# One core, a state space and gated feed-forward layer with its gradients: loads and stores moved to Sync's queue from the 11th group, and the parameter steps spread anew

## The chip, the cores and the metric

The kernel runs on one core of a Trainium2 chip. The metric is device microseconds of one execution; lower is better. The kernel before takes 1762.47 us, the median of three runs (1759.99 to 1764.7).

## The reference

`reference` is a forward pass with its vector-Jacobian product. With x of 2048 tokens by D = 576, and F = 4608:

```
xn  = layernorm(x)
s   = conv(xn, K) + xn * Dskip        # K[d,l] = Re sum_n C[d,n] exp(dt*A[d,n]*l) dt*B[d,n], causal, by FFT; N = 128
g   = silu( (silu(xn @ w1) * (xn @ w3)) @ w2 )
out = x + s * g
```

It returns out and the gradients for grad_out: of x (out_1), of the state space parameters A, B, C, log_dt and Dskip (out_2 to out_9), and of w1, w3, w2 (out_10, out_11, out_12). All of them are bf16. The part that matters here is the backward pass: with go the gradient at the feed-forward's output, the gradients of the hidden values need go @ w2^T, the weight gradients are products over the 2048 tokens (h^T go for w2, xn^T times the gradients of the gate G and of U for w1 and w3), and the input's gradient is the product of those two with w1^T and w3^T. The gradients of A, B, C and log_dt need sums over time of products of the gradient of K with tables.

## The kernel before, in words

The forward pass comes first and stores the gate G and the up product U in DRAM (`G_dram`, `U_dram`). Then `backward` (line 1521) runs. It has two passes that matter here.

The first is the **gradient pass**, the loop `for gi in range(NG)` at line 1599: 18 groups of FG = 256 columns of F each, counted 0 to 17. The 11th group is gi = 10. A group does the following, in stages that the generator `phase6_group` (1743) names as it yields:

- "h0" to "h3": `make(s)` multiplies go with w2T into `ph` (line 1765), ScalarE copies it (1768), VectorE multiplies it into `gu_n` and `gg_n` (1783), which become the gradients of U and G.
- at "h1" and "h3" `phase6_grad2` (1793) makes the gradient of w2, 128 rows at a time (matmuls at 1806, copies at 1810), and stores it (1811).
- at "h3" the load of `h_n` (U of group gi + 2) is issued (`phase6_load_h`, 1688), into the buffer that this group's second `phase6_grad2` has just read.
- "stored": four stores of `gu_n` and `gg_n` to `GU_dram` and `GG_dram` have been issued on Sync's queue (1788).
- "out_11_0" to "out_10_3", "out_11", "out_10": `phase6_grad13` (1813) makes the gradients of w3 and w1 (1826), each with one store (1832), and the rest of 64 rows each (1836, 1838), whose two stores (`tail`, 1843) are issued when the next group's loads are.
- in between, `phase6_prep` (1724) makes the next group's `gu_n`, `gg_n` and `h_n` ready: ScalarE's Silu and its derivative (1733, 1736), products on VectorE (1729, 1730). It begins at "h3" and reads the load of G, `gg_n` (`phase6_load_gg`, 1704), which is issued with the next group's loads (`phase6_load`, 1709).

The buffers `gg_n`, `h_n` and `gu_n` come in pairs, so group gi + 1 loads where group gi - 1 has been read for the last time.

Into this loop **parameter steps** are mixed (`param_step`, 1230): 36 chunks of 16 channels, two steps a chunk, 72 in all. A step (`param_half`, 1393) is eight matmuls of `qT` with `gz` into `et_ps` (1400), then twice a product with `pz` on VectorE (1405) and a reduction (1408). `et_ps` has three buffers and a step uses two. A chunk's loads (`param_loads`, 1379) are a transpose of `qT`, two loads of `gz` and one of `pz`, all on Sync's queue; after a chunk's second step the chunk two further on is loaded. Steps are taken from gi = GP = 11 on: five a group ("h1", "h3", "out_11", "out_10", "end"), and one more at "stored" in groups 12 to 15. The last group has five. That makes 39; the other 33 lie in the second pass. When 8, 16, 24, 32 and all 36 chunks are done, `phase5_blocks` (1450) finishes blocks of channels, a part at each call of `phase5_step`, with loads and stores on POOL's queue.

The second is the **input pass**, `phase6_inputs` (1852): 16 tiles of 128 tokens, each 72 x 2 matmuls of `acts` (transposed loads of `GG_dram` and `GU_dram`) with w1^T and w3^T (1876). The weights come in by DMA transposes, of which `wA` is loaded at "end" of groups 11 to 15 (`load_wT_rows`, 1673) and the rest in groups 16 and 17 (`load_piece`, 1668). Steps are taken at the places in `stops` (1910).

**The order of the work.** A planner sorts the instructions of each engine by priority (`at`) and by when it thinks their inputs are ready; this order is fixed in the program. Where `issue_after` is used, an instruction stands behind a named one. `gp` and `sc` chain all that goes through them on POOL's and ScalarE's queues. `sp` does so on Sync's queue only while `self.chain` is set, which is from gi = 11 on. A DMA's wait for its data or its buffer is done by the issuing queue, so what stands behind it in that queue waits too. Before the change POOL's queue carries the loads of `gg_n` and `h_n` and all stores of weight gradients; Sync's carries the transposes, the chunk loads, the rows of w2 and the GU/GG stores.

Of the kernel before, what the change touches and what calls it, by code (L numbers as in the profile page):

```python
# [17 lines left out]
P = 128  # L18
# [82 lines left out]
class K:  # L101
# [1128 lines left out]
    def param_step(self):  # L1230
        nch = self.cfg.D // 16
        if self.half == 2 * nch:
            return
        if self.half == 0:
            for ch in range(2):
                self.loaded[ch] = self.param_loads(ch)
        ch, dg = divmod(self.half, 2)
        with self.tc.issue_after(self.pe_last.ins):
            self.param_half(ch, dg, *self.loaded[ch])
        if dg == 1 and ch + 2 < nch:  # L1240
            if self.hold is None:
# [279 lines left out]
    def backward(self, T0, TG, TQ, TC, TX, gctx, mats):  # L1521
        nc, cfg = self.nc, self.cfg
        D, L, LT, F, FT = cfg.D, cfg.L, cfg.LT, cfg.F, cfg.FT
# [9 lines left out]
        FA, GP = 14, 11  # L1533
        with ExitStack() as out:
# [22 lines left out]
            self.tail = None  # L1557
            self.at(T0 - TG)
            gg = self.phase6_load_gg(0, inp)
# [128 lines left out]
    def phase6_load_h(self, gi, T, inp):  # L1688
        self.at(T)
        hn = inp.tile([P, self.cfg.LT, self.FG], BF16, name="h_n")  # L1690
        self.gp(lambda: self.nc.gpsimd.dma_start(out=hn[:], in_=self.U_dram[gi]))
        self.hn[gi] = hn
# [11 lines left out]
    def phase6_load_gg(self, gi, inp):  # L1704
        gg = inp.tile([P, self.cfg.LT, self.FG], BF16, name="gg_n")
        self.gp(lambda: self.nc.gpsimd.dma_start(out=gg[:], in_=self.G_dram[gi]))
        return gg
# [85 lines left out]
    def phase6_grad2(self, gi, fl, hn, gwp, ps_gw):  # L1793
# [6 lines left out]
        if True:  # L1800
# [10 lines left out]
            self.gp(lambda: nc.gpsimd.dma_start(out=aps["out_12"][fi * P:(fi + 1) * P, :], in_=gw2[:]))  # L1811

    def phase6_grad13(self, gi, gg_n, gu_n, gwp, ps_gw):
# [7 lines left out]
        for (nat, oname) in ((gu_n, "out_11"), (gg_n, "out_10")):  # L1821
            gw = gwp.tile([P, nfull, FG], BF16, name="gw13", tag="gw13")
            for c in range(nfull):
# [6 lines left out]
                if (oname, c) in (("out_11", 2), ("out_10", 1)):  # L1830
                    yield oname
            self.gp(lambda: nc.gpsimd.dma_start(out=aps[oname][0:nfull * P, fb:fb + FG].rearrange("(c p) f -> p c f", p=P),
                                                in_=gw[:]))
# [9 lines left out]
        def tail():  # L1843
            self.gp(lambda: nc.gpsimd.dma_start(out=aps["out_10"][nfull * P:D, fb:fb + FG], in_=gw[0:rem, :]))
            self.gp(lambda: nc.gpsimd.dma_start(out=aps["out_11"][nfull * P:D, fb:fb + FG], in_=gw[rem:P, :]))
# [6 lines left out]
    def phase6_inputs(self, T2, TX, wT, acts, pool):  # L1852
# [7 lines left out]
        with pool(name="l_sb", bufs=2) as sb, pool(name="l_s1", bufs=1) as s1, \  # L1860
# [43 lines left out]
            for i in range(LT):  # L1904
# [5 lines left out]
                stops = () if i in (0, 1, LT - 1) else (12, 28, 44, 62) if i == 2 else (14, 38, 62) if i in (3, 4, 6, 8) else (20, 50)  # L1910
# [146 lines left out]
```

## Time and profile before

| | |
|---|---|
| median of three runs | 1762.47 us |
| the profiled execution | 1769.46 us |
| its span, first to last instruction | 1767.7 us |
| TensorE matmul busy | 1638.5 us (93%) |
| VectorE busy | 1357.2 us (77%) |
| ScalarE busy | 937.2 us (53%) |
| POOL busy | 352.2 us (20%) |
| Sync's DMA queue (q1) | 282.62 MB, 63.4% of 16 engines' span |
| POOL's DMA queue (q0) | 107.99 MB, 18.9% |

The profile is one execution. In its rows PE is TensorE's matmuls, PEld its weight loads, DVE VectorE, ACT ScalarE, POOL GpSimd and SP Sync; a q behind the name is the engine's queue or sequencer. A row of instructions begins with the start in us and the time, or with the line and ends with the count; idle time of the engine ahead of an instruction stands in square brackets, with what ended it. A row of a stretch gives its length, then busy us and count of each engine, the granted clock of TensorE, the mean busy share of the DMA engines (packets overlap, so it goes over 1) and GB/s. A row of a wait gives us in total, times, and the longest. A row of a DMA issue gives the count, KB each and the median us from issue to landing. A time written as +n is us after the start of its group, which is the end of the last matmul of line 1838 of the group before.

### The profile page before, as it was taken

The numbers are of one execution on the slowest core, as the hardware profiler recorded it, in microseconds if no ns is written. First come the engines' busy times: TensorE is split into PE (matmuls) and PEld (weight loads), VectorE is DVE, ScalarE is ACT, GpSimd is POOL, SyncE is SP. The second block draws the span as 40 slices with busy tenths as digits, with TensorE's granted clock in tenths as the row PEclk, the third lists the DMA queues.
The fourth block names the chain that finished last, engine by engine and source line by source line (L and its number), as shares of the span: only waits on it lengthen the run. The fifth ranks groups of instructions, "written<-read, shape, count | busy, mean of one in ns | idle before, by whom it ended". The sixth has DMA issues, their size and how long they took to land. (4 is left out here: it accounts for less than half of the span.)

```text
span 1767.7 us, 35373 instructions
## 1 busy us (share of the span) xinstructions
PE 1638.5 (93%) x13849; PEld 1206.2 (68%) x13909; DVE 1357.2 (77%) x2102; ACT 937.2 (53%) x1757; POOL 352.2 (20%) x579
## 2 busy tenths in 40 slices
PE   7789988999999999999989899999789997999998
PEld 2445544544535777788878788888678875778886
DVE  8768888795783554988966989569779975878675
ACT  5789999976863112776746676564444510000101
POOL 3112222223134110111111101111001143031132
PEclk9999999999999999999999999999889998999999
DMA  7889998889699988867664756689989999999992
GB/s 222 271 267 366 348 355 304 305 267 298 224 276 236 227 209 183 223 205 217 192 188 156 221 167 214 176 236 242 183 227 251 207 257 212 227 245 208 236 226 50
DMA packets 634718, 411.98 MB, mean 233 GB/s; under 512 B 424422, under 2 KB 579542, under 8 KB 629942
## 3 DMA queue, kind: packets, MB, share of 16 engines
q1 hardware_dynamic: 579676, 282.62, 63.4%
q0 software_dynamic: 32128, 107.99, 18.9%
q10 hardware_dynamic: 22746, 19.10, 3.9%
q8 instruction: 109, 1.79, 0.4%
q14 instruction: 59, 0.48, 0.1%
HBM read 130.88 MB, written 190.89 MB: 182 GB/s over the span
## 5 line engine op out<-in xcount | busy, mean ns | idle before, releaser
L1876 PEld LDWEIGHTS <-acts 128*128 128x128 bf16 x2304 | 225.9, 99 | 68.5 <-DMA acts<-GU_dram 6.8
L1826 PEld LDWEIGHTS <-xn_bf 128*128 128x128 bf16 x2304 | 224.5, 98 | 47.6 <-issue 21.1
L1405 DVE TENSOR_TENSOR pr_q<-et_ps,pz 128x1024 f32<-128x1024 f32 x144 | 175.8, 1221 | 43.0 <-PE et_ps L1400 36.1
L1876 PE MATMUL px<-wT,acts 128*128 128x288 bf16 x1472 | 189.3, 286 | 0.0
L1032 PEld LDWEIGHTS <-xnT 128*128 128x128 bf16 x1152 | 107.0, 98 | 112.2 <-issue 24.2
L1408 DVE TENSOR_REDUCE S_all<-pr_q 128x32 f32<-128x1024 f32 x144 | 175.1, 1216 | 3.1
L1765 PE MATMUL ph<-w2T,goT 128*128 128x256 bf16 x1440 | 174.6, 275 | 3.1 <-ACT gh L1768 3.1
L1032 PE MATMUL pg<-wmB_w,xnT 128*128 128x512 bf16 x545 | 149.1, 379 | 7.4 <-ACT g_t L1048 4.5
L1765 PEld LDWEIGHTS <-goT 128*128 128x128 bf16 x1440 | 140.6, 99 | 21.6 <-issue 4.5
L1806 PE MATMUL pgw<-go_o,h_n 128*128 128x288 bf16 x1152 | 151.8, 287 | 0.2 <-DVE h_n L1730 0.2
L1826 PE MATMUL pgw<-gu_n,xn_bf 128*128 128x256 bf16 x1152 | 136.8, 274 | 15.0 <-ACT gw L1810 13.3
L1032 PE MATMUL pu<-wmB_w,xnT 128*128 128x512 bf16 x553 | 149.9, 379 | 0.8
L1826 PE MATMUL pgw<-gg_n,xn_bf 128*128 128x256 bf16 x1152 | 130.8, 273 | 1.3 <-ACT gw L1828 1.3
L1806 PEld LDWEIGHTS <-h_n 128*128 128x128 bf16 x1152 | 112.4, 98 | 28.2 <-DVE h_n L1730 0.7
L1768 ACT CAST gh<-ph 128x512 bf16<-128x512 f32 x144 | 82.5, 603 | 89.9 <-PE ph L1765 79.9
L1876 PE MATMUL px<-wA,acts 128*128 128x288 bf16 x832 | 112.2, 293 | 10.2 <-DMA acts<-GU_dram 6.5
L1046 ACT ACTIVATE s_t<-pg 128x512 bf16<-128x512 f32 x144 | 88.0, 611 | 58.0 <-PE pu L1040 32.7
L679 ACT ACTIVATE cs_k<-et_ps 128x512 bf16<-128x512 int16 x216 | 111.6, 640 | 0.7 <-PE et_ps L677 0.7
L1932 ACT ACTIVATE go<-gx 128x576 bf16<-128x576 f32 x16 | 10.9, 683 | 189.7 <-DVE gx L1915 157.8
L1811 POOL DMA_DIRECT2D out_dram<-gw x36 | 19.8, 550 | 381.0 <-ACT gw L1810 200.3
L1729 DVE TENSOR_TENSOR gg_n<-gg_n,h_n 128x1024 bf16<-128x1024 bf16 x72 | 48.8, 683 | 57.0 <-ACT gg_n L1736 57.0
L1060 POOL DMA_DIRECT2D U_dram<-u_t x72 | 51.8, 720 | 203.6 <-ACT u_t L1051 196.7
(317 smaller groups left out, 3272.5 us busy)
## 6 DMA issues: line engine op xcount, KB each, us to landing
U_dram<-u_t POOLq DMA_DIRECT2D x72, 256.0 KB, 4.8
H_dram<-h_t SPq DMA_DIRECT2D x72, 256.0 KB, 4.9
G_dram<-g_t POOLq DMA_DIRECT2D x72, 256.0 KB, 5.0
Q_dram<-q_k SPq DMA_DIRECT2D x36, 512.0 KB, 4.7
gg_n<-G_dram POOLq DMA_DIRECT2D x18, 1024.0 KB, 5.8
h_n<-U_dram POOLq DMA_DIRECT2D x18, 1024.0 KB, 8.8
GG_dram<-gg_n SPq DMA_DIRECT2D x36, 512.0 KB, 10.1
GU_dram<-gu_n SPq DMA_DIRECT2D x36, 512.0 KB, 5.2
```

What stands on the lines that cost most here:

```text
L679: self.sin_last = nc.scalar.activation(out=CS[:, :, o:o + 256], in_=pt[:].bitcast(I16)[:, :, 0::2], func=ACT.Sin, scale=6.283184 / 2 ** 16)
L1032: ins = nc.tensor.matmul(pt[:], lhsT=xnT[:, c, ts], rhs=wm[w][:, c, :], start=(q == 0 and c == 0), stop=(q == 1 and c == nfull - 1))
L1046: nc.scalar.activation(out=s_t[:, :, q, :], in_=pgv, func=ACT.Silu)
L1060: self.u_stores[step] = nc.gpsimd.dma_start(out=dst[fb * ng:(fb + 1) * ng, :, i0:i0 + NT, :].rearrange("g p t f -> p g (t f)"), in_=src[:] ...
L1405: nc.vector.tensor_tensor(out=pr[:].rearrange("p r k e -> p r (k e)"), in0=T[x][:].rearrange("p z k h j a -> p (z k h j a)")[:, None].to_b ...
L1408: nc.vector.tensor_reduce(out=self.S_all[:].rearrange("p r (h c) -> p r h c", h=2)[:, :, :, d0:d0 + 2], in_=pr[:].rearrange("p r k (h j a) ...
L1729: nc.vector.tensor_tensor(out=gg[:, sl, :], in0=gg[:, sl, :], in1=hn[:, sl, :], op=ALU.mult)
L1765: self.pe_last = nc.tensor.matmul(ph[j][:, k, :].rearrange("p (a f) -> p a f", f=P), lhsT=lw, rhs=rh, start=(n == 0), stop=(n == nfull))
L1768: self.sc(lambda: nc.scalar.copy(out=gh[:, j], in_=ph[j][:]))
L1806: self.pe_last = nc.tensor.matmul(pgw[pi_][:, 0:pw], lhsT=hn[:, tt, fl * P:(fl + 1) * P], rhs=go_o[:, tt, po:po + pw], start=(tt == 0), st ...
L1826: self.pe_last = nc.tensor.matmul(pw_[:, 0:FG], lhsT=self.xn_bf[:, tt, c * P:(c + 1) * P], rhs=nat[:, tt, :], start=(tt == 0), stop=(tt == ...
L1876: self.pe_last = nc.tensor.matmul(px[pi_][:, 0:pw], lhsT=acts[i][:, ai, fi, :], rhs=w[:, po:po + pw], start=(n == 0), stop=(n == len(steps ...
```

## The change

From the 11th group on (gi = 10) until the gradient pass ends, a flag `one_queue` is set together with `chain`. While it is set,

- the loads of `h_n` and `gg_n` go to Sync's queue. The load of `gg_n` is kept back until stage "h0" of the group (`gg_due`);
- the stores of out_10, out_11 and out_12 (and the tails) go to Sync's queue through `grad_store`, which puts them on a list; `stores_due` issues the list at the start of the next stage;
- all that goes through `sp` is chained one group earlier, and so w2T is loaded two groups ahead from gi = 10 on.

The loads of the first two chunks are issued at "stored" of gi = 10, not with the first step. Steps are taken at "out_10" and "end" of gi = 10, five times in groups 11 to 16, and five times in the last group; the one at "stored" of groups 12 to 15 is gone. That makes 37. In the input pass tiles 5 and 7 have three stops where they had two: 35.

```diff
@@ param_step
-        if self.half == 0:
-            for ch in range(2):
-                self.loaded[ch] = self.param_loads(ch)
@@ backward
+            self.one_queue, self.gg_due, self.due = False, None, []
...
-                self.chain = gi >= GP
+                self.chain = self.one_queue = gi >= GP - 1
...
                 for stage in group if gi == 0 else self.phase6_group(gi, cur, elp, gwp, ps_h, ps_gw):
+                    self.stores_due()
+                    if stage == "h0" and self.gg_due:
+                        self.gg_due()
+                        self.gg_due = None
...
                     if stage == "stored":
-                        c = gi - GP
-                        if c in (1, 2, 3, 4):
-                            step()
+                        if gi == GP - 1:
+                            for ch in range(2):
+                                self.loaded[ch] = self.param_loads(ch)
...
-                    elif stage in ("h1", "h3", "out_11", "out_10", "end") and gi >= GP and not (lastg and stage in ("out_10", "end")):
+                    elif stage in (("out_10", "end") if gi == GP - 1 else ("h1", "h3", "out_11") if lastg else
+                                   ("h1", "h3", "out_11", "out_10", "end") if gi >= GP else ()):
                         step()
...
+            self.one_queue = False
+            self.stores_due()
@@ phase6_load_h
-        self.gp(lambda: self.nc.gpsimd.dma_start(out=hn[:], in_=self.U_dram[gi]))
+        if self.one_queue:
+            self.sp(lambda: self.nc.sync.dma_start(out=hn[:], in_=self.U_dram[gi]))
+        else:
+            self.gp(lambda: self.nc.gpsimd.dma_start(out=hn[:], in_=self.U_dram[gi]))
@@ phase6_load_gg
+        if self.one_queue:
+            self.gg_due = lambda: self.sp(lambda: self.nc.sync.dma_start(out=gg[:], in_=self.G_dram[gi]))
+        else:
+            self.gp(lambda: self.nc.gpsimd.dma_start(out=gg[:], in_=self.G_dram[gi]))
@@ phase6_grad2 (phase6_grad13 and its tail likewise)
-            self.gp(lambda: nc.gpsimd.dma_start(out=aps["out_12"][fi * P:(fi + 1) * P, :], in_=gw2[:]))
+            self.grad_store(aps["out_12"][fi * P:(fi + 1) * P, :], gw2[:])
+
+    def grad_store(self, out, in_):
+        if self.one_queue:
+            self.due.append(lambda: self.sp(lambda: self.nc.sync.dma_start(out=out, in_=in_)))
+        else:
+            self.gp(lambda: self.nc.gpsimd.dma_start(out=out, in_=in_))
+
+    def stores_due(self):
+        for fn in self.due:
+            fn()
+        self.due = []
@@ phase6_inputs
-                stops = () if i in (0, 1, LT - 1) else (12, 28, 44, 62) if i == 2 else (14, 38, 62) if i in (3, 4, 6, 8) else (20, 50)
+                stops = () if i in (0, 1, LT - 1) else (12, 28, 44, 62) if i == 2 else (14, 38, 62) if 3 <= i <= 8 else (20, 50)
```

More of the change, by code (lines that the diff above doesn't have):

```diff
@@ L1705, in phase6_load_gg @@
         gg = inp.tile([P, self.cfg.LT, self.FG], BF16, name="gg_n")
-        self.gp(lambda: self.nc.gpsimd.dma_start(out=gg[:], in_=self.G_dram[gi]))
+        if self.one_queue:
+            self.gg_due = lambda: self.sp(lambda: self.nc.sync.dma_start(out=gg[:], in_=self.G_dram[gi]))
+        else:
+            self.gp(lambda: self.nc.gpsimd.dma_start(out=gg[:], in_=self.G_dram[gi]))
         return gg
@@ L1831, in phase6_grad13 @@
                     yield oname
-            self.gp(lambda: nc.gpsimd.dma_start(out=aps[oname][0:nfull * P, fb:fb + FG].rearrange("(c p) f -> p c f", p=P),
-                                                in_=gw[:]))
+            self.grad_store(aps[oname][0:nfull * P, fb:fb + FG].rearrange("(c p) f -> p c f", p=P), gw[:])
         pw_ = ps_gw.tile([P, 512], FP32, name="pgw")
@@ L1843, in tail @@
         def tail():
-            self.gp(lambda: nc.gpsimd.dma_start(out=aps["out_10"][nfull * P:D, fb:fb + FG], in_=gw[0:rem, :]))
-            self.gp(lambda: nc.gpsimd.dma_start(out=aps["out_11"][nfull * P:D, fb:fb + FG], in_=gw[rem:P, :]))
+            self.grad_store(aps["out_10"][nfull * P:D, fb:fb + FG], gw[0:rem, :])
+            self.grad_store(aps["out_11"][nfull * P:D, fb:fb + FG], gw[rem:P, :])
         self.tail = tail
```

## The prediction

> **What bounds the kernel now.** I read the page's engine totals first, then busy time by stretch, with the stretches cut at the end of each group's last weight gradient matmul (line 1838), then the waits of TensorE, then the queues at the two large ones.
>
> ```profile
> PE 1638.5 (93%) x13849; PEld 1206.2 (68%) x13909; DVE 1357.2 (77%) x2102; ACT 937.2 (53%) x1757; POOL 352.2 (20%) x579
> core 0: us, PE busy (x) PEld busy (x) DVE busy (x) ACT busy (x) POOL busy (x), PEclk, DMA share, GB/s
> 1124.20:1161.20 37.00, 35.82 (x350) 31.01 (x348) 22.89 (x42) 20.39 (x34) 4.79 (x8) 1.00 0.72 207
> 1161.20:1195.60 34.40, 34.09 (x334) 29.55 (x333) 24.70 (x27) 19.41 (x31) 4.78 (x8) 1.00 0.77 216
> 1195.60:1232.60 37.00, 35.95 (x354) 30.81 (x352) 34.59 (x38) 19.40 (x31) 4.78 (x8) 1.00 1.01 247
> 1232.60:1280.00 47.40, 38.04 (x354) 31.88 (x352) 37.47 (x41) 19.40 (x31) 4.79 (x8) 0.89 1.12 178
> 1280.00:1326.80 46.80, 38.44 (x352) 32.39 (x352) 37.40 (x41) 19.45 (x31) 4.78 (x8) 0.89 0.90 228
> 1326.80:1365.00 38.20, 36.21 (x358) 30.89 (x354) 37.66 (x41) 19.41 (x31) 4.78 (x8) 1.00 0.99 247
> 1365.00:1401.30 36.30, 35.89 (x361) 31.30 (x358) 35.73 (x40) 19.87 (x32) 4.40 (x8) 1.00 0.87 203
> 1401.30:1443.00 41.70, 37.60 (x359) 31.57 (x357) 40.66 (x49) 11.61 (x25) 13.07 (x25) 1.00 1.12 250
> ```
>
> TensorE bounds the whole (93% busy). The eight stretches are groups 10 to 17, counted from 0 as in the code. The steps in them are 0, 5, 6, 6, 6, 6, 5, 5. Group 11, with five, takes 34.4 us and TensorE is idle for 0.3 of them. The groups with six take 37.0 to 47.4, and in them VectorE is nearly always busy: 37.66 of 38.20 us in group 15. So where a group has six steps, VectorE sets the pace.
>
> ```profile
> L1405 DVE TENSOR_TENSOR pr_q<-et_ps,pz 128x1024 f32<-128x1024 f32 x54 | 65.8, 1219 | 19.8 <-PE et_ps L1400 18.0
> L1408 DVE TENSOR_REDUCE S_all<-pr_q 128x32 f32<-128x1024 f32 x54 | 65.6, 1214 | 0.8
> PE pgw L1826 <- ACT gw L1810: 9.1, 5, 8.0
> PE et_ps L1400 <- DVE S_all L1408: 7.3, 1, 7.3
> PE et_ps L1400 <- DVE pr_q L1405: 3.5, 2, 2.5
> 1256.62 1.06 ACT L1733 ACTIVATE gu_n<-gg_n 128x1024 bf16<-128x1024 bf16 x1 [7.75 <-DMA gg_n<-G_dram]
> 1258.01 3.57 PE L1826 MATMUL pgw<-gu_n,xn_bf 128*128 128x256 bf16 x16 [8.01 <-ACT gw L1810]
> 1287.36 0.58 PE L1400 MATMUL et_ps<-gz,qT 128*128 128x128 bf16 x4 [7.30 <-DVE S_all L1408]
> 1232.96 0.55 POOL L1706 DMA_DIRECT2D gg_n<-G_dram  x1 [0.70 <-DVE S_all L1408]
> 1239.63 19.56 SPq L1686 DMA_TRANSPOSE wA<-in_B_w_dram  x2
> DMA to landing us min/median/max: 5.7/7.0/23.6
> ```
>
> A step is two products and two reductions, 2 x (1.219 + 1.214) = 4.87 us of VectorE. The third wait row is group 17's alone. The story of groups 13 and 14 is in the timeline rows: the G load issued at 1232.96 landed 23.6 us later (the others of groups 11 to 16: median 7.0). ScalarE waited for it, so did its copies behind it, and TensorE stood 8.01 us. VectorE starved meanwhile, then had four steps at once, and TensorE stood 7.30 us for it at the group's end. Both idles are followed by a reduced granted clock (0.89 in both stretches). While the load crept, two transposes for wA held Sync's queue for 19.56 us and the DMA moved 178 GB/s at a share of 1.12: all transfers were slow, not one queue. No other group shows this.
>
> **The change, part by part.**
>
> *Steps.* Groups 12 to 15 lose one each (the one at "stored"), group 10 gains two, tiles 5 and 7 of the last pass gain one each; 72 remain. VectorE needs 37.5 us with six (41 instructions), so 37.5 - 4.9 = 32.6 with five, below TensorE's 34.4. I take group 11's 34.4 plus 0.4 for short waits, 34.8, for groups 11 to 16. Group 17 keeps five steps, but inherits no backlog: its 3.5 us of waits go, 41.7 to 38.2. Groups 12 to 17 took 37.0 + 47.4 + 46.8 + 38.2 + 36.3 + 41.7 = 247.4; they become 5 x 34.8 + 38.2 = 212.2, so -35.2. Group 11 pays +0.4.
>
> ```profile
> 1510.21 0.45 PE et_ps L1400 x8
> 1543.00:1584.00 41.00, 38.38 (x336) 30.93 (x334) 31.37 (x49) 4.53 (x9) 16.24 (x30) 1.00 1.14 241
> 1584.00:1622.00 38.00, 37.96 (x334) 30.83 (x334) 31.20 (x33) 3.29 (x6) 3.61 (x6) 1.00 1.10 227
> ```
>
> A step costs TensorE 0.45 us. Group 10 pays 0.9; its VectorE has 37.0 - 22.89 = 14 us free for the 9.7. The two tiles pay 0.9. Tiles 6 and 7 (second stretch) hold five steps, with VectorE at 31.2 of 38; a sixth makes 36.1, which fits. In tiles 4 and 5 VectorE has 41 - 31.4 = 9.6 us to spare for 4.9, but also the finishing blocks, which now begin two stops later. Between 0 and 4.9 I take +1.0, near the free end, since both stretches have room.
>
> *First loads.* The loads of the first two chunks now stand in Sync's queue behind h_n, the four GU/GG stores and one gradient store, and the first step is wanted after the second G-side matmul block of group 10.
>
> ```profile
> 1146.77 1.19 SPq L1788 DMA_DIRECT2D GU_dram<-gu_n  x2
> 1148.06 4.95 SPq L1788 DMA_DIRECT2D GG_dram<-gg_n  x2
> 1143.70:1161.20 17.50, 17.47 (x173) 15.30 (x173) 5.26 (x8) 11.13 (x17) 2.60 (x4) 1.00 0.99 282
> 1152.22 1.04 PE L1826 MATMUL pgw<-gg_n,xn_bf 128*128 128x256 bf16 x8
> gg_n<-G_dram POOLq DMA_DIRECT2D x6, 1024.0 KB, 7.0
> pz<-PZ_dram SPq DMA_DIRECT2D x17, 256.0 KB, 5.8
> gz<-gK_dram SPq DMA_DIRECT2D x34, 64.0 KB, 3.5
> ```
>
> The step is reached at about 1152.2 + 3.5 = 1155.7 (two blocks of 16 matmuls, one each 0.11 us, since eight take 1.04 with a latency of some 0.27). From 1146.8, where the stores began in the old order, 3.95 MB have to pass before its gz has landed: h_n 1.05, the stores 2.1, out_12 0.15, qT 0.52 (16 x 128 x 128 values of 2 bytes), gz 0.13. At the 282 GB/s of that stretch that is 14.0 us, 1160.8, and with 1.5 us for the landing 1162.3. So TensorE would stand up to 6.6 us, and up to 9 with a reduced clock behind it. It is 0 if the planner, which fixes TensorE's order, puts the step behind later matmuls. I take +4.0, the middle, as no row decides.
>
> *G loads on Sync's queue.* At the end of groups 11 to 15 the order on Sync becomes: gradient store, two wA transposes, after groups 12 and 14 a chunk's four loads too, two tail stores, the G load. The deadline is in the rows of group 13: ScalarE stood from 1256.62 - 7.75 = 1248.9 on, that is 16.3 us after the group's start, and TensorE from 1258.01 - 8.01 = 1250.0, +17.4.
>
> ```profile
> 1198.97 7.43 SPq L1686 DMA_TRANSPOSE wA<-in_B_w_dram  x2
> 1206.52 2.37 SPq L1686 DMA_TRANSPOSE qT<-Q_dram  x1
> 1208.94 1.23 SPq L1386 DMA_DIRECT2D gz<-gK_dram  x2
> ```
>
> In group 12 wA's issue ended at 1206.4, +10.8. The G load behind it lands 5.7 us later at best, at +16.5; but wA then no longer shares the DMA with 1 MB of G, some 3.7 us at 282 GB/s, which gives +12.8. Groups 12, 14 and 16: in time, 0. Groups 13 and 15 have 2.37 + 1.23 + 0.5 = 4.1 us more before it: +16.9 to +20.6, so 0 to 4.3 us late each. I take 1.0 each, +2.0 (0 to 8.6), nearer the low end because no POOL traffic is beside it.
>
> *h_n loads and stores.*
>
> ```profile
> 1181.25 0.54 POOL L1691 DMA_DIRECT2D h_n<-U_dram  x1
> 1184.57 1.07 SPq L1788 DMA_DIRECT2D GU_dram<-gu_n  x2
> ```
>
> Sync now waits at h_n until TensorE has done the second out_12 product, and the GU/GG stores are queued behind it. In group 11 POOL issued h_n at +20 and Sync the stores at +23.4, so the order was this one already, and the readers of GU/GG come in the last pass. The stores of out_12, out_11 and out_10 stand behind whatever Sync holds; their buffers are wanted again half a group later or more. 0. POOL is freed of about 4.8 us a group, and nobody waited for it: 0.
>
> *Sum.* -35.2 + 0.4 + 0.9 + 0.9 + 1.0 + 4.0 + 2.0 = -26.0. Against the profiled execution's own 1769.46 us that is 1743.5. The median of the three timed runs is 1762.47, 7.0 lower. If all runs hold the slow stretch, it is 1762.5 - 26.0 = 1736.5. If they lack it, groups 13 and 14 took about 38 each there, not 94.2 together, 18.2 of the gain were never to be had, and it is 1754.7. The middle is 1745.6; I say **1745**.
>
> **A rule weighed.** By the share row of group 12 (1.01 at 247 GB/s) the DMA engines are already near full with two queues, and the G loads landed in 7.0 us beside 7.43 us of transposes. The Trainium skill, "DMA: Bandwidth & Descriptors", section "Queues, rings and completion order", says each DMA engine goes round-robin between the queue rows that have work, a packet each. By that rule a G load gives up a turn of its own when it moves to Sync's row, and the sum gets the high ends of the G load term, 8.6 in place of 2.0, 1751.6; by the rows it stays at 1745.
>
> **The rivals.**
>
> *Sync's single queue becomes the bound (slower).*
>
> ```profile
> DMA packets 95172, 52.48 MB, mean 219 GB/s; under 512 B 62699, under 2 KB 90347, under 8 KB 93739
> q1 hardware_dynamic: 91643, 35.29, 72.7%
> q0 software_dynamic: 3504, 16.85, 21.9%
> ```
>
> These rows are groups 11 to 16. Without four steps' loads (0.45 MB each) 50.7 MB remain, 8.44 MB a group, and 34.8 us ask for 243 GB/s from what is nearly one queue. At the old mean of 219 a group takes 38.5 us: 6 x 3.7 = +22 and some 3 in group 17, so 1745 + 25 = 1770. It decides from 8.44 MB / (34.8 + 17.5/6 us) = 224 GB/s down. For it: 247 is the best group so far. Against it: the 219 holds the slow stretch of 20 us, and 282 was reached in group 10. Chance 0.18.
>
> *The slow stretch was this execution's alone and the first step waits in full.* 1754.7 + 5 + the 6.6 of late G loads = 1766: no change that can be told. For it: profile 7.0 us above the median. Chance 0.12.
>
> *The planner hides the first step and the G loads come in time.* 1745 - 6 = 1739, faster. Chance 0.15.
>
> **How the numbers follow.** Chances: the forecast (1734 to 1757) 0.55, the third rival 0.15, no change 0.12, the bound queue 0.18. A timing can tell 0.3%, 5.3 us, from no change: faster below 1757.2 (0.55 + 0.15 = 0.70), same 0.12, slower above 1767.8 (0.18). The low end 1731 is the third rival where all runs hold the stretch (1736.5 - 6); the high end 1768 leaves most of the bound queue out. The likeliest case's own range goes 2 us beyond 1736.5 and 1754.7.
>
> **What would show it.** Right: groups 11 to 16 at 34.4 to 36 us, no wait of TensorE on S_all over 1 us, VectorE busy under 34 us a group. First loads: a wait of L1400 on gz or qT in group 10. G loads: a landing later than +16 after a group's start, with ScalarE's L1733 waiting on it. Bound queue: DMA share at 1.0 or more in every group and G landings drifting later from group 12 on. The forecast is wrong if the late G load comes back in several groups, or if the last pass loses more than 5 us to the moved steps.

## The result, and the profile after

| | before | after |
|---|---|---|
| median, six runs each | 1764.46 us | 1786.30 us |
| the profiled execution | 1769.46 us | 1784.0 us |
| its span | 1767.7 us | 1782.2 us |

The ratio of the runs is 1.0118, 95% interval 1.0073 to 1.0163. A second comparison, eleven runs against thirty, gave 1.0096 (1.0052 to 1.0140). The change costs about 1%, 17 to 21 us; 1745 was forecast, 1.0% faster.

The profile after, first the engine totals of its page, then busy time by stretch for groups 10 to 17, cut and with the columns as in the prediction:

```profile
PE 1645.1 (92%) x13849; PEld 1210.0 (68%) x13909; DVE 1358.1 (76%) x2102; ACT 937.5 (53%) x1757; POOL 313.6 (18%) x516
...
1131.50:1174.20 42.70, 38.27 (x362) 32.51 (x361) 24.76 (x44) 20.54 (x34) 0.00 (x0) 0.96 0.70 185
1174.20:1209.20 35.00, 34.69 (x340) 30.14 (x340) 31.97 (x34) 19.42 (x31) 0.00 (x0) 0.99 0.86 222
1209.20:1245.30 36.10, 35.06 (x347) 30.44 (x346) 33.11 (x37) 19.42 (x31) 0.00 (x0) 1.00 0.93 238
1245.30:1289.60 44.30, 37.30 (x347) 31.48 (x346) 33.17 (x37) 19.42 (x31) 0.00 (x0) 0.92 0.83 206
1289.60:1327.10 37.50, 35.05 (x347) 30.43 (x346) 33.09 (x37) 19.43 (x31) 0.00 (x0) 1.00 0.97 239
1327.10:1370.70 43.60, 37.71 (x347) 31.88 (x346) 33.06 (x37) 19.42 (x31) 0.00 (x0) 0.92 0.77 201
1370.70:1405.50 34.80, 34.80 (x348) 30.49 (x347) 34.18 (x38) 19.52 (x31) 0.00 (x0) 1.00 0.99 230
1405.50:1444.90 39.40, 37.00 (x358) 31.32 (x359) 38.39 (x47) 11.63 (x25) 9.37 (x18) 1.00 1.02 230
```

VectorE (third busy column) is relieved, 33.1 us a group where it had 37.5. But groups 13 and 15 take 44.3 and 43.6 us with TensorE's clock at 0.92, and group 10 takes 42.7 in place of 37.0. TensorE's waits in these groups:

```profile
PE pgw L1848 <- ACT gw L1821: 16.8, 6, 7.0
PE et_ps L1397 <- DMA gz<-gK_dram: 3.2, 1, 3.2
PE et_ps L1397 <- DVE pr_q L1402: 1.4, 1, 1.4
```

The first is TensorE's product with `gu_n` standing for ScalarE's copies, the second the first step standing for its `gz`. The copies are late because ScalarE stands for G, and G is late because of what is ahead of it on Sync's queue. The timeline around the start of group 13 (1245.3), other engines' rows cut but for a few:

```profile
1243.31 2.76 SPq L1691 DMA_TRANSPOSE qT<-Q_dram  x1
...
1245.26 0.62 PE L1397 MATMUL et_ps<-gz,qT 128*128 128x128 bf16 x8
...
1246.12 1.22 SPq L1383 DMA_DIRECT2D gz<-gK_dram  x2
1247.38 0.58 SPq L1386 DMA_DIRECT2D pz<-PZ_dram  x1
...
1248.06 0.94 SPq L1826 DMA_DIRECT2D out_dram<-gw  x2
1249.05 4.41 SPq L1691 DMA_TRANSPOSE wA<-in_B_w_dram  x2
...
1252.89 1.22 DVE L1402 TENSOR_TENSOR pr_q<-et_ps,pz 128x1024 f32<-128x1024 f32 x1
...
1253.56 3.23 SPq L1691 DMA_TRANSPOSE qT<-Q_dram  x1
...
1256.84 1.23 SPq L1383 DMA_DIRECT2D gz<-gK_dram  x2
1258.16 0.53 SPq L1386 DMA_DIRECT2D pz<-PZ_dram  x1
...
1258.80 1.14 SPq L1826 DMA_DIRECT2D out_dram<-gw13t  x2
1259.99 0.58 SPq L1715 DMA_DIRECT2D gg_n<-G_dram  x1
...
1266.32 1.28 ACT L1744 ACT_TABLE_LOAD   x1 [6.71 <-DMA gg_n<-G_dram]
1267.61 1.06 ACT L1744 ACTIVATE gu_n<-gg_n 128x1024 bf16<-128x1024 bf16 x1
1269.01 3.57 PE L1848 MATMUL pgw<-gu_n,xn_bf 128*128 128x256 bf16 x16 [6.96 <-ACT gw L1821]
```

The G load is issued at +14.7 us of the group. The transfer is quick, 6.3 us until ScalarE runs, but ScalarE has stood for 6.7 us and TensorE then for 7.0. When the group begins, the queue is still issuing a chunk's loads. Behind them come the stores, `wA`, and the loads of a second chunk, which take the buffers of the chunk that the "end" step has finished.

None of these loads stands still for that step. Its matmuls are the row at 1245.26, its last product is the row at 1252.89, which ends at 1254.1, and the `qT`, `gz` and `pz` behind `wA` are issued at 1253.6, 1256.8 and 1258.2. A wait shows as a gap between two rows of the queue, as in the kernel before, where `w2T` starts at 1173.92, 9.6 us behind the end of the row ahead of it. Here no gap is over 0.11 us from 1194.4 to 1265.4: the queue issues one DMA right behind the other.

Against the first profile of before the span is 14.5 us longer: -4.3 in groups 10 to 17 (317.7 to 313.4), +11.3 in the input pass (326.0 to 337.3), +7.6 up to the end of group 0 (747.6 to 755.2), where nothing was changed. Which of these are real, further profiles had to tell.

### The profile page after: what moved, and what is told of

Read it like the earlier page. It is cut to its first block, busy times and chain, and to the rows that moved or that the text cites. A ratio compares the mean times of both kernels' runs of the same rounds, so it can differ in the third digit from the quotient of the medians.

```text
span 1782.2 us, 35350 instructions
## 1 busy us (share of the span) xinstructions
PE 1645.1 (92%) x13849; PEld 1210.0 (68%) x13909; DVE 1358.1 (76%) x2102; ACT 937.5 (53%) x1757; POOL 313.6 (18%) x516
## 5 line engine op out<-in xcount | busy, mean ns | idle before, releaser
L1848 PE MATMUL pgw<-gu_n,xn_bf 128*128 128x256 bf16 x1152 | 137.0, 276 | 22.6 <-ACT gw L1821 20.7
L1897 PE MATMUL px<-wA,acts 128*128 128x288 bf16 x832 | 112.3, 292 | 12.9 <-DMA acts<-GU_dram 9.3
L1054 DVE TENSOR_TENSOR h_t<-s_t,u_t 128x1024 bf16<-128x1024 bf16 x72 | 49.3, 685 | 57.1 <-ACT u_t L1051 57.0
L1828 POOL DMA_DIRECT2D out_dram<-gw x40 | 26.2, 655 | 349.9 <-ACT gw L1850 171.6
```

The lines of the kernel that those rows point to most:

```text
L1054: nc.vector.tensor_tensor(out=h_t[:].rearrange("p t (g f) -> p g t f", g=ng), in0=s_t[:], in1=u_t[:], op=ALU.mult)
L1848: self.pe_last = nc.tensor.matmul(pw_[:, 0:FG], lhsT=self.xn_bf[:, tt, c * P:(c + 1) * P], rhs=nat[:, tt, :], start=(tt == 0), stop=(tt == ...
L1897: self.pe_last = nc.tensor.matmul(px[pi_][:, 0:pw], lhsT=acts[i][:, ai, fi, :], rhs=w[:, po:po + pw], start=(n == 0), stop=(n == len(steps ...
```

## The experiments

My theory after the result (A): the relief of VectorE is real, and G's place on Sync's queue eats it. Rivals: the new steps are at fault (B), or one queue is too slow for the bytes (C). All edits are against the changed kernel. "Groups 12-15" and "10-17" are us of the profile. "Issue 13 / 15" is when G was issued in these groups after their start, "Silu 13 / 15" when ScalarE began its first Silu on it.

| run | ratio to before (95%) | 10-17 | 12-15 | issue 13 / 15 | Silu 13 / 15 | input pass |
|---|---|---|---|---|---|---|
| before, 1st profile | 1 | 317.7 | 169.4 | 0.3 / 0.3 | 24.0 / 16.2 | 326.0 |
| e5, before | 1.0028 (0.9985-1.0071) | 299.6 | 151.1 | 0.3 / 0.3 | 16.5 / 16.2 | 346.0 |
| e14, before | one run | 300.7 | 152.5 | 0.3 / 0.3 | 16.2 / 18.1 | 332.0 |
| after | 1.0118 (1.0073-1.0163) | 313.4 | 161.5 | 14.7 / 13.9 | 22.3 / 21.2 | 337.3 |
| e6, after | 1.0096 (1.0052-1.0140) | 311.3 | 159.2 | 14.4 / 13.8 | 21.5 / 20.9 | 346.1 |
| e1 steps only | 0.9946 (0.9906-0.9986) | 288.8 | 142.2 | 0.3 / 0.3 | 15.6 / 15.6 | 333.3 |
| e11 steps only | 0.9933 (0.9893-0.9974) | 288.8 | 142.2 | 0.3 / 0.3 | 15.6 / 15.6 | 338.9 |
| e2 queue only | 1.0035 (0.9998-1.0072) | 311.1 | 161.0 | 13.2 / 10.3 | 20.9 / 17.1 | 335.4 |
| e3 G on POOL | 1.0005 (0.9972-1.0037) | 293.4 | 142.2 | 1.3 / 2.0 | 15.6 / 15.7 | 357.0 |
| e4 stores on POOL | 1.0021 (0.9982-1.0059) | 301.6 | 147.2 | 11.3 / 10.3 | 18.1 / 15.8 | 341.8 |
| e7 first loads early | 1.0081 (1.0045-1.0118) | 311.7 | 160.7 | 15.8 / 12.9 | 22.9 / 20.2 | 344.1 |
| e8 wA at "stored" | 1.0083 (1.0045-1.0122) | 310.8 | 158.5 | 13.8 / 13.9 | 20.9 / 21.3 | 341.2 |
| e9 "end" step behind G | 0.9973 (0.9932-1.0014) | 298.2 | 146.8 | 9.8 / 8.5 | 16.4 / 15.6 | 347.8 |
| e10 e9 and e7 | 0.9957 (0.9915-1.0000) | 295.2 | 148.9 | 11.6 / 9.0 | 18.3 / 15.7 | 327.4 |
| e12 e3 and e7 | 0.9958 (0.9920-0.9996) | 290.1 | 143.4 | 1.1 / 3.7 | 15.6 / 17.0 | 343.2 |
| e13 e9, e7 and e8 | 0.9960 (0.9919-1.0000) | 291.3 | 145.0 | 7.9 / 8.6 | 15.6 / 15.6 | 333.2 |

**Each half alone.** e1 takes the new steps and leaves the queues as they were, Sync's chain from group 11 on included:

```diff
-                self.chain = self.one_queue = gi >= GP - 1
+                self.chain = gi >= GP
```

> The new step schedule alone: two steps in group 10, five in groups 11 to 17, three stops in tiles 5 and 7, the first two chunks' loads at "stored" of group 10; all loads of G and U and all gradient stores stay on POOL's queue. Theory A (the loss is the G load behind Sync's queue, and the relief of VectorE was real): groups 12 to 16 take 34.4 to 36 us each, no TensorE wait on gw copies over 1 us, groups 10 to 17 together about 290 us against 317.7 in the profile of before; if the input pass keeps its +11, the time is about 1764 - 28 + 11 = 1747, if not, about 1737. Theory B (the relief was not real: groups of five are slow for another reason, such as the DMA share): groups 12 to 15 stay above 37 us on the mean and the time is 1764 or more. The input pass tells whether its +11 belongs to the steps: +11 here if the two moved stops cost it, 0 if the moved stores and loads do.

Groups 12 to 15 of e1, by stretch:

```profile
1202.50:1238.04 35.54, 35.23 (x347) 30.47 (x347) 33.13 (x37) 19.42 (x31) 4.80 (x8) 1.00 0.99 256
1238.04:1273.58 35.54, 35.23 (x345) 30.45 (x346) 33.14 (x37) 19.42 (x31) 4.81 (x8) 1.00 0.96 244
1273.58:1309.12 35.54, 35.23 (x346) 30.46 (x346) 33.13 (x37) 19.42 (x31) 4.80 (x8) 1.00 1.07 253
1309.12:1344.68 35.56, 35.24 (x347) 30.46 (x347) 33.16 (x37) 19.42 (x31) 4.80 (x8) 1.00 0.92 239
```

TensorE is idle for 0.3 us a group, as the relief promised, and the kernel is 0.5% faster than before. Theory B falls. By the ratio its time is 1755 us, where 1737 to 1747 had been expected: the base of that sum was the first profile of before, slow stretch included. e11 is the same kernel again:

> The new step schedule alone once more, beside the others and with a second profile: 0.5% faster than before, groups 10 to 17 at 289 us. Its input pass (333.3 us in the first profile, between 326 and 346 in two profiles of before) shows what three stops in tiles 5 and 7 cost beside the scatter: under 3 us if my +1.9 holds, so a value between 326 and 349.

It has the same groups to 0.1 us and a ratio of 0.9933. It is the one changed kernel that was measured twice, both times with 1 outside the interval.

e2 moves the queue and keeps the old steps (the four changes to steps, stops and first loads undone):

```diff
@@ param_step
+        if self.half == 0:
+            for ch in range(2):
+                self.loaded[ch] = self.param_loads(ch)
@@ backward
                     if stage == "stored":
-                        if gi == GP - 1:
-                            for ch in range(2):
-                                self.loaded[ch] = self.param_loads(ch)
+                        c = gi - GP
+                        if c in (1, 2, 3, 4):
+                            step()
...
-                    elif stage in (("out_10", "end") if gi == GP - 1 else ("h1", "h3", "out_11") if lastg else
-                                   ("h1", "h3", "out_11", "out_10", "end") if gi >= GP else ()):
+                    elif stage in ("h1", "h3", "out_11", "out_10", "end") and gi >= GP and not (lastg and stage in ("out_10", "end")):
...
@@ phase6_inputs
-                stops = () if i in (0, 1, LT - 1) else (12, 28, 44, 62) if i == 2 else (14, 38, 62) if 3 <= i <= 8 else (20, 50)
+                stops = () if i in (0, 1, LT - 1) else (12, 28, 44, 62) if i == 2 else (14, 38, 62) if i in (3, 4, 6, 8) else (20, 50)
```

> The queue move alone: from group 10 on the loads of G and U and the gradient stores on Sync's queue, Sync chained from group 10; the steps as before (none in group 10, six in groups 12 to 15). Theory A: Sync's queue holds a sixth step's share of chunk loads too, so G lands later than with five: groups 12 to 15 lose 5 to 10 us each against a time of 37 to 38 without a late load, and the time is 1764 + 15 to 30, 1780 to 1795. Theory B (the queue move is harmless and the new steps cost the time): 1764 within 5. If the input pass is again 11 us longer than in the profile of before, that part belongs to the queue move.

In the profile the loss is there: groups 12 to 15 take 161.0 us against 151.1, with G late again in 13 and 14 (42.17 and 42.63 us). It is smaller than expected, and by the time, 1.0035 with 1 inside the interval, it can't be told from none. With six steps these groups already wait for VectorE, 38.0 us each, and part of the lateness may lie beside that wait. The two halves do not add: +11.5 us for the queue and -10.8 for the steps in groups 10 to 17, but +11.7 to +13.8 together (all against 299.6).

**Before again.** The base of these sums is a second and a third profile of the kernel before:

> The kernel before once more, for a second profile. Theory E (the slow stretch of groups 13 and 14 was that execution's alone): all G loads land within 13 us of the group's start, groups 12 to 15 take 37 to 38 us each, groups 10 to 17 together about 299.5 us, 18 less than in the first profile, so that 18 of the 35 us of relief were never to be had. Theory F (it belongs to the kernel): a G load lands after +16 again, a group of over 45 us, and a sum near 317. The input pass of 326.0 us and the start of the gradient pass at 749 tell how much of the differences of +11 and +7.6 lies within what executions of one kernel differ by: within 3 us if these are real differences.

> The kernel before a third time, for its profile: groups 13 and 14 at 38 us each and groups 10 to 17 at 299.6 us if the slow stretch was the first execution's alone; the input pass between 326 and 346 us, as in the two profiles there are, if it scatters by about 20 us from execution to execution.

Groups 13 and 14 of e5:

```profile
1235.68:1273.68 38.00, 35.89 (x352) 30.87 (x352) 37.46 (x41) 19.44 (x31) 4.81 (x8) 1.00 1.03 247
1273.68:1311.70 38.02, 36.04 (x355) 30.94 (x355) 37.48 (x41) 19.44 (x31) 4.80 (x8) 1.00 1.01 251
```

The slow stretch (47.4 and 47.0 us) was the first execution's alone among these three: theory E. The input pass of before, in the first profile and in e5:

```profile
1441.70:1767.70 326.00, 304.46 (x2585) 243.65 (x2585) 227.78 (x317) 32.30 (x63) 88.94 (x163) 0.97 0.98 203
```

```profile
1426.57:1772.60 346.03, 308.43 (x2585) 245.49 (x2585) 227.52 (x317) 32.40 (x63) 89.02 (x163) 0.96 1.02 191
```

One program differs by 20 us there between two executions, so the +11.3 of the first pair proves nothing. All profiles lie between 326 and 357, and those with the new steps overlap those with the old. The end of group 0 lies between 747.5 and 755.5 us after the start in all of them; +7.6 is within that.

**The changed kernel again,** for the same reason:

> The changed kernel once more beside the two kernels below, for a second profile. Theory A: G lands after +18 in groups 13 and 15 again, both take 42 to 45 us, group 10 takes 42 to 43 with a wait of some 3 us on gz, and TensorE waits again about 4 us for gz in tile 5 of the input pass. If the late loads are scatter, they lie in other groups or are gone. Time 1780 to 1790.

Unlike the slow stretch, the late loads are reproducible: issued at +14.4 and +13.8, 43.8 and 42.2 us. The 4 us wait for `gz` in tile 5 did not come back; waits of 1.0, 2.5 and 2.8 us for `gz` lay at other places of the input pass.

**One transfer taken off Sync's queue.** e3 leaves G on POOL's queue, e4 the gradient stores:

```diff
@@ phase6_load_gg (e3)
-        if self.one_queue:
+        if False:
@@ grad_store (e4)
-        if self.one_queue:
+        if False:
```

> The changed kernel with one thing undone: the load of gg_n stays on POOL's queue, issued with the next group's loads. Theory A (place in Sync's queue makes G late): G lands within 8 us of the group's start, the waits of 7.0, 2.4 and 5.9 us on gw copies in groups 13 to 15 and the two stretches of half clock go, groups 12 to 15 take 34.5 to 36 us, and the time is 1786 - 22 = 1764. Theory C (all transfers are too slow beside so much traffic, whatever the queue): G takes over 12 us to land and the time stays within 5 of 1786.

> The changed kernel with the gradient stores of out_10, out_11 and out_12 back on POOL's queue; the loads of G and U stay on Sync's. Theory A: what stands before the G load on Sync's queue is mostly wA and a chunk's loads, the four stores issue in about 2 us together, so G comes 2 us earlier at most: groups 13 and 15 gain up to 2 us each and the time is 1780 to 1786. Theory D (the stores' waits for ScalarE hold the queue and make G late): G lands in time in groups 13 and 15 and the time is about 1766. If the input pass gets its 11 us back, its loss came from the stores on Sync.

e3 brings groups 12 to 15 back in full, 142.2 us, with the same bytes moving. Theory C, that all transfers are too slow, falls. The kernel as a whole is then level with before, 1.0005; its group 10 still took 42.0 us, and its input pass, 357.0 us, was the longest of all.

e4 was expected to bring 2 us a group. It brought G forward by 3.4 and 3.6 us and groups 13 and 15 back by 6.4 and 8.0, and its time, 1.0021, is nearer to the 1766 us that I had put down for theory D (the stores wait in the queue). But the rows above hold no gap that would be such a wait. The stores in them issue in 2.1 us, but from one G load to the next (1220.4 to 1260.0) all stores together take 4.0 us, and in a queue without gaps each of them delays G. A load that is just late is cheap: what counts is how far behind ScalarE's turn it lands. Group 10 of e4 took 45.1 us, the longest of all.

**What holds the queue.** The first loads moved up (e7), then `wA` (e8), then the "end" step (e9), each alone:

```diff
@@ e7: first two chunks' loads
+                    if stage == "h1" and gi == GP - 1:
+                        for ch in range(2):
+                            self.loaded[ch] = self.param_loads(ch)
                     if stage == "stored":
-                        if gi == GP - 1:
-                            for ch in range(2):
-                                self.loaded[ch] = self.param_loads(ch)
@@ e8: wA
-                    if stage == "end" and 0 <= gi - GP < cfg.DT:
+                    if stage == "stored" and 0 <= gi - GP < cfg.DT:
@@ e9: the step of "end" at "h0" of the next group, behind gg_due()
-                    elif stage in (("out_10", "end") if gi == GP - 1 else ("h1", "h3", "out_11") if lastg else
-                                   ("h1", "h3", "out_11", "out_10", "end") if gi >= GP else ()):
+                    elif stage in (("out_10",) if gi == GP - 1 else ("h0", "h1", "h3", "out_11") if lastg else
+                                   ("h0", "h1", "h3", "out_11", "out_10") if gi >= GP else ()):
```

> The changed kernel with one thing moved: the loads of the first two chunks are issued at "h1" of group 10, ahead of h_n, the GU/GG stores and the first gradient store on Sync's queue, not at "stored" behind them. Theory A (my term of the first loads): the wait of 3.25 us on gz in group 10 and the half clock behind it go, group 10 takes 37.5 to 38.5 us in place of 42.7, and the time falls by about 4 us, to 1782. If group 10 stays above 41, the two steps cost it in another way.

Group 10 fell from 42.7 to 37.7 us, the wait on `gz` is gone. But group 11 went from 35.0 to 39.15: G was now issued at +12.2 there, where it had been +9.1, and TensorE stood 2.9 us for it. The loads had only changed places with something else on the same queue.

> The changed kernel with one thing moved: the two transposes for wA are issued at "stored" of groups 11 to 15 and not at "end", so they stand behind the GU/GG stores and no longer ahead of the next group's G load on Sync's queue. G stays on that queue. Theory A (G is late because of what is issued ahead of it): G is issued 4 to 7 us earlier, in groups 13 and 15 at +7 to +10, lands by +16, groups 12 to 15 take 35 to 36.5 us each, and the time falls by 16 to 20 us, to about 1767. Theory C (one queue is too slow for the traffic, wherever the transposes stand): the transposes delay the gradient stores and the chunk loads instead, G still lands after +18 in groups 13 and 15, and the time stays within 5 us of 1786.

A miss for theory A as I put it, and what I had written for theory C there came about: G was issued no earlier in group 15 and only 0.9 us earlier in group 13, and Silu began after +20 in both. Sync's queue of e8 around the start of group 13 (1240.90):

```profile
1237.77 4.46 SPq L1691 DMA_TRANSPOSE wA<-in_B_w_dram  x2
1242.33 1.92 SPq L1691 DMA_TRANSPOSE qT<-Q_dram  x1
1244.30 1.34 SPq L1383 DMA_DIRECT2D gz<-gK_dram  x2
1245.68 0.58 SPq L1386 DMA_DIRECT2D pz<-PZ_dram  x1
1246.36 0.94 SPq L1826 DMA_DIRECT2D out_dram<-gw  x2
1247.39 3.12 SPq L1691 DMA_TRANSPOSE qT<-Q_dram  x1
1250.57 1.53 SPq L1383 DMA_DIRECT2D gz<-gK_dram  x2
1252.20 1.21 SPq L1386 DMA_DIRECT2D pz<-PZ_dram  x1
1253.51 1.14 SPq L1826 DMA_DIRECT2D out_dram<-gw13t  x2
1254.70 0.58 SPq L1715 DMA_DIRECT2D gg_n<-G_dram  x1
```

From 1190.5 to 1259.9 no gap of this queue is over 0.3 us. That is why e8 brought nothing: `wA` goes out earlier, but still ahead of G, and in a queue that never runs empty that only pushes the chunk behind it back. The second `qT`, from 1247.39, is still ahead of G with its `gz` and `pz`. The "end" step that frees its buffers had ended its matmuls at 1241.5 and its last product at 1249.7, ahead of the `qT` (1247.39) and the `pz` (1252.20) that need them.

At the time I read this otherwise. The view of the queue's waits puts 2.8 us of the second `qT`'s issue down to a step's matmuls (L1397), and I changed the theory to A2: G stands behind loads that wait for work of the new group. But the matmuls that end within that issue, 1249.58 to 1250.19, are those of the next step, which this load does not need, and the rows show no gap. The order of the loads, which e9 changes, is a question of its own.

> The changed kernel with the step of "end" taken at "h0" of the next group instead, right behind the issue of the G load, so that no chunk loads, which wait for that step's TensorE and VectorE work, stand ahead of G on Sync's queue. G, U and the stores stay on that queue, and wA stays ahead of G. Theory A2 (G is late because the queue ahead of it waits in order for the "end" step, not because of bytes): G is issued at +5 to +9 in groups 12 to 15, Silu begins by +16 in all of them, no TensorE wait on gw copies over 1.5 us, groups 12 to 15 take 35.5 to 36.5 us each and groups 10 to 17 about 294 in place of 311 to 313. Theory C (one queue is too slow): G still lands after +18 in groups 13 and 15, or the chunk loads come late instead and TensorE waits for gz, and the sum stays over 305.

Sync's queue of e9 at the start of group 13 (1240.41):

```profile
1244.13 4.43 SPq L1691 DMA_TRANSPOSE wA<-in_B_w_dram  x2
1248.66 1.48 SPq L1826 DMA_DIRECT2D out_dram<-gw13t  x2
1250.24 0.53 SPq L1715 DMA_DIRECT2D gg_n<-G_dram  x1
1250.88 4.42 SPq L1691 DMA_TRANSPOSE qT<-Q_dram  x1
```

G is issued at +9.8 in place of +14.7, and the 4.8 us between are about the issue time of the second chunk's four loads (5.2 us in the rows after), which now stand behind it. Groups 13 and 15 take 36.2 and 35.7 us. Of the 19.3 us that groups 12 to 15 had lost against the steps alone (161.5 - 142.2), 14.7 came back. Group 14 alone stayed clearly late, +12.6 and 39.1 us, with 2.6 us of waiting on TensorE. A2 as put down was met in part: G came by +9 in group 15 alone, and groups 10 to 17 took 298.2 us and not 294.

> Both orders on Sync's queue mended, everything still on it: the step of "end" at "h0" behind the G load, and the first two chunks' loads at "h1" of group 10. Theory A2: groups 10 to 17 take 288 to 291 us, as with the new steps alone (288.8), and the time is that of the new steps alone. Theory C: groups 12 to 15 stay above 38 us on the mean.

> The changed kernel with the G load back on POOL's queue and the first two chunks' loads at "h1" of group 10; the U loads and all gradient stores stay on Sync's queue. It differs from the new steps alone by those. My terms of 0 for them hold if groups 10 to 17 take 288 to 291 us and the time is within 5 us of the new steps alone; if the stores or the U load hold up others, the sum is over 295.

> All three orders on Sync's queue mended, everything still on it: the step of "end" at "h0" behind the G load, the first two chunks' loads at "h1" of group 10, and wA at "stored". Theory A2 (only the order of the queue makes G late): G is issued by +8 in groups 12 to 15 and Silu begins by +16.0 in all of them, groups 12 to 15 take 35.5 to 36 us each and groups 10 to 17 together 288 to 291 us, as with the new steps alone (288.8). Theory C2 (what is left of the lateness in the two kernels mended before is the one queue's own backlog: it runs late whatever stands where): G is still issued after +10 in two or more of the groups 12 to 15 and their sum stays at 146 or more against 142.1 with the new steps alone.

e10 and e13 put the orders together. e10 fell short of A2's 288 to 291 us (295.2; its group 13 took 39.7 with G at +11.6). e13 came to 291.3 with everything still on Sync's queue, 20.0 us under e6 in groups 10 to 17. It lies between the two theories put down for it: groups 12 and 14 still had G issued at +10.6 and +11.6 and took 36.32 and 37.23 us, as C2 said, but groups 12 to 15 took 145.0 us, under its 146. In group 14 of e13 `wA` and a chunk's loads stand ahead of G without a gap from 1275.0 on. So both the gain and the rest of about 2.5 us are issue time ahead of G: the order decides most of it, as A2 said, though not by waits, and the queue's own backlog, C2, is that rest. What makes one `qT` take 1.9 us to issue and another 4.4 was not tried.

e12 shows that the U loads and the stores on Sync's queue cost next to nothing by themselves: 290.1 against 288.8 us, where group 15 gave 1.2 to one late `gz`.

## Why the prediction was wrong

**The step that failed is the term "G loads on Sync's queue", +2.0 us (0 to 8.6).** Groups 12 to 15 show 17.0 (e6) to 19.3 us (after) more than with the new steps alone. Its mechanism, G late behind `wA` and a chunk's loads, stood in the prediction, and the places too, groups 13 and 15; three numbers in it were wrong.

1. *The landing.* I put G at +16.9 at best: `wA` issued by +7.1 (10.8 less 3.7, because it would be quicker alone), 4.1 us of chunk loads, 5.7 us to land. ScalarE began at +21.0. By the rows of group 13, `wA` ends at +8.1, the chunk's loads take 5.2 us, the two tail stores, which I had listed and not counted, 1.3, and G 6.3. So the discount was about right (`wA` took 4.4 us in place of 7.4), and that the upper end, +20.6, came close is luck: it left out both the discount and the stores. Behind these sizes lies a question that I did not ask, how full the queue is. The issues of Sync's queue fill 255.8 of the 313.4 us of groups 10 to 17, and from 1194.4 to 1265.4 they leave no gap over 0.11 us, so each DMA ahead of G delays it by its whole issue.
2. *The deadline.* I took +16.3, where ScalarE stood in the slow group 13 of before, with its table load (1.28 us) already done. In a group that is not late it turns to G 0.7 us earlier. In e1, with group 13 beginning at 1238.04, the table load starts at +14.3 and Silu at +15.6. And in group 13 after, the table load itself stands for G (1266.32, in the rows above), which is the other 1.3 us. So G was wanted at +14.3:

```profile
1252.33 1.28 ACT L1744 ACT_TABLE_LOAD   x1
1253.62 1.06 ACT L1744 ACTIVATE gu_n<-gg_n 128x1024 bf16<-128x1024 bf16 x1
```

3. *The price of being late.* While the clock stays at 1.00, a late Silu costs about its lateness (Silu at +18.1 in place of +15.6 in e4: 37.9 in place of 35.5 us). When TensorE's stop is followed by the reduced clock, that comes on top. Group 13 after: Silu 6.7 us late, 8.8 us longer. The 6.9 us behind the stop ran at a clock of 0.67, which is 6.9 x (1 - 0.67) = 2.3 us, and 6.7 + 2.3 = 9.0. It can come sooner: in group 14 of e9 Silu was 2.4 us late, and with the clock at 0.96 the group took 3.6 us longer. I charged the clock for the first loads and forgot it here.

**The relief of VectorE, -35.2.** Right in kind: 33.1 us a group, and no wait on `S_all` is left. But 18.2 us of it were the slow stretch, which one of three profiles of before has. I saw the question and took the middle of 1736.5 and 1754.7; the runs, not one profile, are what the change is measured against, and 1754.7 was the end to start from. The rest was 4.9 us smaller: groups 10 to 17 of e1 are 10.8 us shorter than in e5, and 35.2 - 18.2 - 0.4 - 0.9 = 15.7 was predicted. Groups 12 to 15 take 35.5 us and not 34.8, group 17 39.4 and not 38.2. Another 1.3 us were a misreading: I ended group 17 of before at 1443.0, and its last matmul of line 1838 ended at 1441.7.

With these the account closes: 1754.7 + 4.9 + 15.0 to 17.3 (G) + 1.0 (first loads) = 1775.6 to 1777.9, where the ratios 1.0096 and 1.0118 times 1762.5 give 1779 and 1783, each with 8 us to either side. It closes within that noise only: e2 has the same groups 10 to 17 (311.1 us) at a ratio of 1.0035, so some microseconds of the changed kernel's loss may lie outside these groups, and no run settles where.

**The first loads, +4.0,** were right in size, with some luck: group 10 takes 42.7 and 43.1 us with them late, 37.7 without (e1, e7), so 5.0 to 5.4. (In e1 they are issued at "stored" too, but Sync is not chained in group 10 there, and `gz` went out at 1143.7, ahead of the stores.) The place was not right: the planner put the step at +36.0 and not +31.5, and `gz` came at +39.3 and not +38.1, after two GG stores ahead of it had taken 7.3 us of the queue (from 1155.57) and `qT` 3.3. The 1.5 us in that sum for the landing stand in no row; here TensorE began 1.9 us after the issue of `gz` ended.

**h_n and the stores, 0.** e12 bears that out for the groups. But the stores also stand ahead of G, and without them (e4) groups 12 to 15 get back 14.3 us (161.5 to 147.2). A step that costs nothing by itself was part of the cost of another.

**Tiles 5 and 7, +1.9.** Not settled. e1 and e11 are 9.5 and 11.9 us faster than before by their ratios (0.0054 x 1768.2, 0.0067 x 1774.5) and 10.8 us by their groups, so there is room for +1.3 or -1.1, and the ratios have 7 us to either side; the input pass scatters by 20 us.

**The rivals.** The first, "Sync's single queue becomes the bound", had the sign and the queue, but not the measure: it was to decide below 224 GB/s, with a DMA share of 1.0 or more and G drifting later from group to group. The late groups do move 201 to 206, but as an effect, at shares of 0.77 to 0.83, and G is latest in 13 and 15 and in time in 16. e9 moves the same bytes through the same queue in another order at 241 GB/s and more in groups 12 to 14. The queue was full in issue time, long before it was full in bytes, and then its order decides which load is late. The second rival was right in its first half (the slow stretch) and too low in its price for the late loads (6.6). The planner did not hide the first step in full (3.25 us of stop) and G was late: the third falls.

**The rule weighed.** The round robin of the Trainium skill ("DMA: Bandwidth & Descriptors", "Queues, rings and completion order") would have made G's transfer slower. It was not: 6.3 us from issue to ScalarE's start in group 13, beside 7.0 as the median on POOL's queue. All of the delay is ahead of the issue. The Trainium skill says on the same page, in "Issuing engines are not separate DMA queues", that issuing from several engines only saves the sequencer's time to start a DMA, usually small beside the DMA itself. Here the measurement differs: G's issue alone back on POOL's queue (e3) gave 17.0 to 19.3 us in four groups. One start is indeed short, 0.58 us for G, but G first had to let the starts ahead of it pass, 14.7 us of them from the start of group 13 on.

## What to carry to other kernels

A DMA that is moved to another engine's queue inherits all that stands ahead of it there, the issue times as well as the waits. Before moving one, list that queue's rows with their issue times around the place where the load will stand, and look for the gaps. Where there are none, the queue is full: moving another DMA forward brings nothing as long as it stays ahead of the load (e8), and putting the load ahead of others brings their issue time (e9). What the view of waits calls a wait of such a queue is one only where its rows show a gap. Take the deadline from a stage that is not late, add the clock's penalty from about 2.5 us of a stop of TensorE on, and profile the kernel before more than once before a slow stretch is counted as gain. The best version here is the new step schedule with the queues left alone, 0.5% to 0.7% faster than before; by their times e10, e12 and e13 (0.9957 to 0.9960) can't be told from it.

## What was not expected of the hardware

- The input pass of one program took 326, 346 and 332 us in three executions. Between the first two TensorE's waits for `acts` and `gz` grew from 11.2 to 22.6 us, one of them 9.9 us at a place where the first had none. Groups 10 to 12 of e5 and e14 agree within 0.01 us. What makes the transfers of the input pass scatter was not tried.
- A stop of TensorE of 2.4 us left the clock at 1.00 (group 14 after), and stops of 3.0 us and more were followed by a lower one (e10 group 13, 3.02 us: 0.96; group 10 after, 3.25 us: 0.96). Between them it fell either way: 2.92 us gave 0.96 in group 11 of e7 and 2.99 us gave 1.00 in its group 14. In group 17 of the kernel before, the same stop of 2.55 us left 1.00 in the first profile and gave 0.96 in e5. The Trainium skill ("TensorE: Matmul & The Clock Gate", "What's actually happening") tells of an idle window of about 3.4 us that runs freely. That the same stop is followed by either fits a window that runs freely; 2.55 us is shorter than the window, and there the measurement differs.
